# A state-space layer and a memory transformer on one core: a branch for the fallback, a last output tile in three pieces, x in half rows

## The chip, the core and the metric

The kernel runs on one core of a Trainium2 chip. The time is that of the device in microseconds for one execution; lower is better. TensorE (PE) multiplies, VectorE (DVE), ScalarE (ACT) and GpSimd (POOL) do elementwise work, SyncE (SP) issues most transfers; ACT issues a few.

## The reference

Two independent computations stand side by side in the output's last axis. Part A is a linear recurrence over 2048 steps with 1024 complex states. Part B is attention over segments of 32 tokens, 32 heads of 128, where each segment sees 8 memory rows that are the first 8 output rows of the segment before. Cut to what matters:

```python
# part A: x is (1, 2048, 1024)
Bu = einsum('bld,pd->blp', x, B_bar)
for t in range(L):
    h = Lam_bar * h + Bu[:, t, :]
y = 2.0 * einsum('blp,dp->bld', hseq, Cmat).real + x * Dskip
# part B: 64 segments of 32 rows
for s in range(n_seg):
    h = concatenate([mem, x[:, 32*s:32*s+32, :]], axis=1)
    q, k, v = (einsum('btd,dhe->bhte', h, W) for W in (Wq, Wk, Wv))
    p = softmax(where(mask, q @ k.T * scale, -1e9))
    o = einsum('bhte,hed->btd', p @ v, Wo)
    mem = o[:, :8, :]
    outs.append(o[:, 8:, :])
return concatenate([a, b], axis=-1)      # (1, 2048, 2048), bf16
```

## The kernel before

Part B is computed with guessed memory rows for all segments at once, and a check compares the guess with what came out. The check writes a flag of one number. If it is set, `general` computes part B again, segment by segment; with the inputs given it isn't. The fallback is a loop at the very end, `For_i(0, f0 * NSEG, 1)` at L1063, that runs 64 times or no time at all. Its body holds 164 matmuls, 84 of them in an inner loop over heads.

The stages, in order of time:

1. Values. Seven matmuls of constants open the program (L907). Four tiles of 128 rows of x (L371, `load_rows`) and the first block of Wv (L405, `load_wv`) come by plain transfers on two queues, SP's and ACT's. TensorE turns each x tile by eight multiplications with the identity (L378, `turn_rows`), VectorE copies the result to `b_xe`, and `v_first` multiplies it with the eight chunks of Wv (L413): two chunks after the first x tile, six matmuls after the second, ten after the third, fourteen after the fourth. The order of these is pinned. The second Wv block, four small parameter loads and the rest of x, by transposing transfers on SP (L368), are issued behind them. The rest of the values follow (L413), mixed with part A's first product (L256).
2. Part A's second product (L310) with part B's guess. In it, `zeros` stores zeros to small gaps of the scratch arrays in HBM, 24 transfers on SP.
3. Queries, keys and attention (L584, L567, L610, L628).
4. The output product (L684): 16 tiles of 128 rows, each in two halves of 512 columns, 32 heads accumulated in one PSUM tile, so 32 matmuls of 128x512 each half. `evac` copies a half to SBUF, on DVE or ACT (L77, L75), and stores both halves together on SP (L714). The last tile is treated apart: each half is copied as two quarters of 256 columns, the first by DVE and stored by SP, the second by ACT and stored by ACT (L710). The check's matmuls stand between the tiles 4 to 7 of this stage.
5. The flag is loaded into a register of each engine (L1062), then the loop at L1063.

Part of the order is written out by hand (`keep_in_program_order`), the rest is by priority of the program's order. Every transfer is given one of eight semaphores in turn and waits, before it is issued, for the transfer that had that semaphore before it, the eighth before. At the loop each engine checks and settles these semaphores, jumps over the body, and checks again.

Of the kernel before, what the change touches and what calls it, by code (L numbers as in the profile page):

```python
# [9 lines left out]
BF16 = mybir.dt.bfloat16  # L10
# [13 lines left out]
T = 2048; D = 1024; KC = 8; TT = 16  # L24
PC = 8; TB = 512; NB = 4
H = 32; E = 128; SEG = 32; M = 8; NSEG = 64; L = M + SEG
# [9 lines left out]
NM = NTL + NMX  # L36
# [280 lines left out]
class PartB:  # L317
# [32 lines left out]
    def zeros(self, pool):  # L350
        k = self.k
        z = pool.tile([32, 128], BF16, name="b_z", bufs=1)
        k.G.memset(z[:], 0.0)

        def put(dst, n):
            k.tc.keep_in_program_order(k.SP.dma_start(dst.rearrange("p (a n) -> p a n", a=4), z[0:n].unsqueeze(1).to_broadcast([n, 4, 128])))
        for hb in range(HB):
            put(self.vx[hb][64 + NMX:GX, :], GX - 64 - NMX)
            put(self.vx[hb][T + 32:NSLOT, :], 32)
            put(self.omd[NM:MT, hb * 512:(hb + 1) * 512], MT - NM)  # L360

    def load_x(self, c0, c1):

# [335 lines left out]

    def evac(self, t, half):  # L700
        k = self.k
        if t not in self.ost and t < TT - 1:
            self.ost[t] = self.p4.tile([128, D], BF16, name="b_ost", bufs=5)
        acc = self.acc.pop((t, half))
        if t == TT - 1:
            r, o = slice(t * 128, (t + 1) * 128), D + 512 * half
            for i in range(2):
                st = self.p4.tile([128, 256], BF16, name="b_oe", bufs=4)
                k.copy("vs"[i], st[:], acc[:, 256 * i:256 * i + 256])
                (k.SP if i == 0 else k.nc.scalar).dma_start(self.out[0, r, o + 256 * i:o + 256 * i + 256], st[:])  # L710
            return
        k.copy("s" if half else "v", self.ost[t][:, half * 512:half * 512 + 512], acc)
        if half:
            k.SP.dma_start(self.out[0, t * 128:(t + 1) * 128, D:2 * D], self.ost.pop(t)[:])  # L714


    def check(self):
        k = self.k; V, S, PE = k.V, k.S, k.PE
# [142 lines left out]
def kernel_main(tc, A_x, A_Lre, A_Lim, A_Bre, A_Bim, A_Cre, A_Cim, A_logdt, A_Dskip, B_x, B_mem0, B_Wq, B_Wk, B_Wv, B_Wo, out,  # L861
                force=False, dbg=None):
    with ExitStack() as ctx:
# [16 lines left out]
        with pool("p1", "right") as p1:  # L880
            tmp = a.hsp.tile([128, 2 * PC * TB], BF16, name="a_hs", bufs=4)
            w01 = a.hsp.tile([128, 2 * PC * TB], BF16, name="a_hs", bufs=4)
            wvs = {i: w01[:, 4096 * i:4096 * i + 4096].rearrange("p (a b) -> p a b", a=KC) for i in range(2)}
            st0 = a.hsp.tile([128, 2 * PC * TB], BF16, name="a_hs", bufs=4)
            b.st0 = [st0[:, 1024 * i:1024 * i + 1024].rearrange("p (a b) -> p a b", a=2) for i in range(8)]
            a.pin = b.pin = True
            a.tab = a.wp = a.btp = b.vst = p1
            a.jf = b.rall[:, 0:TB + 1]
            xr = tmp[:, 4096:8192].rearrange("p (t d) -> p t d", t=4)
            q2 = (k.SP, nc.scalar)  # L890
            for j in range(2):
                b.load_rows(0, xr, q2[j], slice(j * 512, j * 512 + 512))
                b.load_wv(0, wvs[0], KC, q2[j], [j])
            for t in range(1, 4):
                b.load_rows(t, xr, q2[t % 2])
                b.load_wv(0, wvs[0], 4, q2[1 - t % 2], [t])
            for j in range(2):
                b.load_wv(1, wvs[1], 2, q2[j], [j])
            a.load_params(tmp)
            k.SP.dma_start(tmp[0:M, 0:D], b.mem0[0])  # L900
            b.load_x(512, 1024)
            b.load_x(1024, 1536)
            b.load_x(1536, T)
            one = nc.const_aps.tensor(1.0, [128, 512], BF16)
            pw = k.ps("O")
            for i in range(7):
                k.PE.matmul(pw[:, i % 2, :], one[:, 0:128], one, start=True, stop=True)  # L907

            def values():
                yield from b.v_first(wvs[0], xr, k.SP)  # L910
                for hb, q in [(1, 0), (1, 1)] + [(hb, q) for q in range(2, 8) for hb in range(2)]:
                    yield from b.v_pair(hb, q, wvs[hb], k.SP)
                for hb in range(2, HB):
                    for q in range(8):
                        if q == 1 and hb + 1 < HB and hb + 1 not in wvs:
                            wvs[hb + 1] = b.load_wv(hb + 1)
                        yield from b.v_pair(hb, q, wvs[hb], k.SP)
            v = values()
            done = 0
            while done < 20:  # L920
                next(v); done += 1
                if done == 7:
                    a.params(p1, tmp)
                    b.init(tmp, k.ps('O')[:, 0, :])
                    a.bt = a.load_b(0)
                    a.load_x(0)
                    tabs = a.tables(0)
                if done == 18:
                    a.load_x(1)
                if done in (9, 14, 17):  # L930
                    next(tabs)
                if done in (11, 13, 15, 17, 19):
                    b.sum_x((done - 11) // 2, p1)
            a.tabs = a.ntabs
            oged = 0
            for n in range(PC * NB):
                pc, tb = n // NB, n % NB
                a.stage1(pc, tb)
                if n in (0, 1):
                    a.load_x(2 + n)  # L940
                    wvs[2 + n] = b.load_wv(2 + n)
                if tb == 1 and pc + 1 < PC:
                    nbt = a.load_b(pc + 1)
                want = 20 + 4 * (n + 1) if n < 4 else 36 + (92 * (n - 3) + 27) // 28
                half = done + 2
                while done < want:
                    next(v, None); done += 1
                    if done == half:
                        a.post(a.prev)
                while done >= 32 and oged < done // 16:  # L950
                    b.og(oged, wvs.pop(oged))
                    oged += 1
                if pc + 1 < PC:
                    if tb == 0:
                        tabs = a.tables(pc + 1)
                    else:
                        next(tabs)
                    if tb == 3:
                        a.tabs, a.bt = a.ntabs, nbt
                if n == 3:  # L960
                    a.pin = b.pin = False
                if n == 8:
                    masks(k)
                    check_consts(k)
                    dB = k.cst.tile([128, D], BF16, name="a_dB")
                    tc.keep_in_program_order(nc.scalar.dma_start(dB[:], A_Dskip.unsqueeze(0).to_broadcast([128, D])))
                if n == 28:
                    a.load_c(0, 0)
                if n == 29:
                    a.load_c(0, 1)  # L970
            a.post(a.last)
            k.V.memset(b.rall[:], 0.0)
            a.load_c(1, 0)
            a.load_c(1, 1)
# [56 lines left out]
        with pool("olb", "right", 5) as olb, pool("p4", "right") as p4:  # L1031
            b.p4 = p4
            b.olp[1] = olb
            for i in range(5):
                b.load_o(*divmod(i + 3, 4))
            for _ in b.op_some([(2, 0), (3, 0)], range(3), "S"):
                pass
            for _ in b.op_some([(0, 1), (1, 1), (2, 1), (3, 1)], range(3), "O"):
                pass
            for half in range(2):  # L1040
                for t in range(4):
                    b.op(t, half, 3)
                    b.evac(t, half)
            ck = b.check()
            for tb in range(1, 4):
                if tb < 3:
                    for q in range(4):
                        b.load_o(tb + 1, q)
                for t in range(4 * tb, 4 * tb + 4):
                    for half in range(2):  # L1050
                        for _ in b.op_some([(t, half)], range(4), "A" if tb > 1 else "S"):
                            pass
                        b.evac(t, half)
                    if tb == 1:
                        for _ in range(3):
                            next(ck, None)
            for _ in ck:
                pass
        rest.close()
        if force:  # L1060
            k.V.memset(b.flag[:], 1)
        f0 = nc.values_load(b.flag[0:1, 0:1], min_val=0, max_val=1)  # L1062
        with tc.For_i(0, f0 * NSEG, 1) as it:  # L1063
            with tc.tile_pool(name="gen", bufs=1) as gp:
                b.general(it, gp)


@with_exitstack
# [59 lines left out]
```

## Time and profile before

| what | us |
|---|---|
| median of 7 runs | 1245.96 |
| lowest, highest | 1244.84, 1247.94 |
| profiled execution, its own time | 1245.16 |
| its span, first to last instruction | 1243.5 |
| TensorE busy | 1231.3 |
| VectorE, ScalarE, GpSimd busy | 610.8, 326.6, 200.2 |
| granted TensorE clock, mean | 0.999 |

A line of the chain of waits says when a piece starts, how long it is, and what it is: work of an engine, a transfer, or issue. A line of an engine's groups gives duration and count. A busy matmul of 512 columns shows 379 ns, but the next starts 216 ns after it: they overlap, and a stretch is best counted from the chain. An engine's name with q is its sequencer, which issues and branches.

### The profile page before, as it was taken

The page shows a single profiled execution, that of the slowest core. Times are in us where ns is not written, and L with a number is a line of the kernel's source. Part 1 is how long each engine was busy: PE and PEld are TensorE (multiplying, and loading weights), DVE is VectorE, ACT ScalarE, POOL GpSimd, SP SyncE. Part 2 cuts the span into 40 slices and gives each one's busy share as a digit, 9 for nine tenths or more (in the row PEclk, how much of TensorE's full clock was granted, in tenths as well). Part 3 has the DMA queues.
Part 4 walks back from the last instruction along what each step waited for, and adds up shares of the span by engine and source line. Part 5 has one row for each costly group of instructions (what it writes and reads, how often), then busy time and mean ns, then how long its engine had stood idle before and what let it go on. Part 6 is the DMA issues. An engine that isn't in the chain of part 4 may idle for free.

```text
span 1243.5 us, 19626 instructions
## 1 busy us (share of the span) xinstructions
PE 1231.3 (99%) x8045; PEld 653.3 (53%) x8116; DVE 610.8 (49%) x1124; ACT 326.6 (26%) x755; POOL 200.2 (16%) x284
## 2 busy tenths in 40 slices
PE   9999999999999999999999999999999999999998
PEld 4444444444455445566666665565556554454443
DVE  4889999999941122444444454444444450011000
ACT  3444434444310001332332333333333330000000
POOL 2000000000032140222222222322232230000000
PEclk9999999999999999999999999999999999999999
DMA  9942232333566559577768554645575469607000
GB/s 226 266 119 68 85 94 68 102 93 79 151 191 201 149 167 170 100 150 150 148 113 182 122 131 95 129 88 87 105 139 105 72 205 237 131 18 153 17 27 18
DMA packets 305733, 153.95 MB, mean 124 GB/s; under 512 B 147048, under 2 KB 299104, under 8 KB 305640
## 3 DMA queue, kind: packets, MB, share of 16 engines
q1 hardware_dynamic: 303832, 150.69, 52.8%
q10 hardware_dynamic: 1808, 1.97, 0.5%
q8 instruction: 65, 1.06, 0.4%
q14 instruction: 28, 0.23, 0.1%
HBM read 73.70 MB, written 44.71 MB: 95 GB/s over the span
## 4 chain that ended last, share of the span: by engine, by line
PE 99%; DMA 0%; issue 0%; ACTq 0%; DVE 0%; ACT 0%
PE psP L584 33%; PE psS L684 10%; PE psP L413 9%; PE psS L413 9%; PE psO L256 9%; PE psP L684 5%; PE psP L310 4%; PE psS L310 4%; PE psP L567 4%; PE psO L628 3%; PE psS L610 3%; PE psO L684 2%; PE psP L504 1%; PE psP L730 1%; PE psO L481 1%; DMA a_hs<-in_B_x_dram 0%
## 5 line engine op out<-in xcount | busy, mean ns | idle before, releaser
L584 PE MATMUL psP<-b_xe,w 128*128 128x480 bf16 x2048 | 439.6, 366 | 0.0
L584 PEld LDWEIGHTS <-w 128*128 128x128 bf16 x2048 | 193.7, 98 | 183.5
L617 POOL TENSOR_TENSOR b_m<-b_e,maskB 99x396 bf16<-99x396 bf16 x160 | 139.6, 872 | 347.9 <-ACT b_e L613 347.9
L77 DVE CAST b_q<-psP 128x480 bf16<-128x480 f32 (+1 forms) x192 | 98.1, 532 | 145.6 <-PE psP L584 134.1
L413 PEld LDWEIGHTS <-b_xe 128*128 128x128 bf16 x1024 | 99.8, 98 | 120.8 <-DVE b_xe L77 1.3
L684 PEld LDWEIGHTS <-b_ol 128*128 128x128 bf16 x1024 | 99.3, 98 | 116.9
L75 ACT ACTIVATE b_k<-psP 128x480 bf16<-128x480 f32 x128 | 73.2, 572 | 318.4 <-PE psP L584 318.4
L613 ACT ACTIVATE b_e<-psS 99x396 bf16<-99x396 f32 x176 | 87.6, 498 | 171.3 <-PE psS L610 164.6
L635 DVE TENSOR_TENSOR b_ot<-psO,b_rall 99x512 bf16<-99x512 f32 x176 | 121.6, 691 | 6.4
L256 PE MATMUL psO<-w,a_bt 128*128 128x512 bf16 x496 | 114.7, 379 | 0.8
L684 PE MATMUL psS<-w,b_ol 128*128 128x512 bf16 x438 | 98.6, 379 | 0.6
L633 DVE RECIPROCAL b_rall<-psO 99x4 f32<-99x4 f32 x176 | 31.1, 177 | 132.9 <-PE psO L628 132.9
L413 PE MATMUL psS<-w,b_xe 128*128 128x512 bf16 x378 | 90.1, 379 | 0.4
L413 PE MATMUL psP<-w,b_xe 128*128 128x512 bf16 x376 | 89.8, 379 | 0.4
L256 PEld LDWEIGHTS <-a_bt 128*128 128x128 bf16 x512 | 49.7, 98 | 59.0
L310 PEld LDWEIGHTS <-a_hs 128*128 128x128 bf16 x512 | 49.5, 98 | 58.3
L77 DVE CAST b_ost<-psS 128x512 bf16<-128x512 f32 x13 | 9.0, 691 | 125.4 <-PE psS L684 125.4
L628 PE MATMUL psO<-b_v,b_m 99*128 99x129 bf16 x704 | 70.4, 221 | 0.0
L610 PEld LDWEIGHTS <-b_k 128*128 128x128 bf16 x704 | 50.0, 98 | 33.9 <-DVE b_k L77 0.2
L610 PE MATMUL psS<-b_q,b_k 128*128 128x99 bf16 x704 | 60.1, 208 | 0.1
L75 ACT ACTIVATE b_vst<-psS 128x512 bf16<-128x512 f32 x56 | 33.4, 597 | 97.5 <-PE psS L413 74.8
L310 PE MATMUL psP<-w,a_hs 128*128 128x512 bf16 x253 | 57.7, 379 | 0.2
(200 smaller groups left out, 1079.9 us busy)
## 6 DMA issues: line engine op xcount, KB each, us to landing
b_v<-b_vx SPq DMA_DIRECT2D x16, 1056.0 KB
b_os<-b_ot SPq DMA_DIRECT2D x16, 960.0 KB
w<-in_B_Wv_dram SPq DMA_DIRECT2D x14, 1024.0 KB
b_vx<-b_vst SPq DMA_DIRECT2D x48, 256.0 KB
w<-in_B_Wo_dram SPq DMA_DIRECT2D x12, 1024.0 KB
w<-in_B_Wq_dram SPq DMA_DIRECT2D x16, 512.0 KB
w<-in_B_Wk_dram SPq DMA_DIRECT2D x16, 512.0 KB
a_xn<-in_A_x_dram SPq DMA_DIRECT2D x32, 128.0 KB
```

Of the source, the lines that this page charges most:

```text
L75: self.S.activation(out, in_, ACT.Copy)
L77: self.V.tensor_copy(out, in_)
L256: m = PE.matmul(u[:, i, :], self.bt[:, i, c, :], self.xT[tb][:, c, :], start=(c == 0), stop=(c == KC - 1))
L310: PE.matmul(py[:], self.hs[tb][:, pc, i, tt * 128:(tt + 1) * 128], self.ct[half, i][:, pc, :], start=(pc == 0 and i == 0), stop=(pc == PC ...
L413: m = self.k.PE.matmul(p[:], self.xe[:, c, t * 128:(t + 1) * 128], w[:, c, :], start=(c == 0), stop=(c == KC - 1))
L584: PE.matmul(p[:, 0:480], w[:, i * KC + c, hh * 128:(hh + 1) * 128], self.xe[:, c, 480 * q:480 * q + 480], start=(c == 0), stop=(c == KC - 1))
L610: PE.matmul(s[:, j * GW:(j + 1) * GW], kt[:, hh, g0:g0 + 128], qt[:, hh, g0:g0 + GW], start=True, stop=True)
L613: k.S.activation(e[:], s[0:GW, 0:4 * GW], ACT.Exp, scale=float(E) ** -0.5, accum_out=self.accE[0:GW, i:i + 1])
L617: k.G.tensor_tensor(v4(m[:, 0:4 * GW]), v4(e[:]), mask[0:GW, :, :].unsqueeze(2).to_broadcast([GW, 2, 2, GW]), ALU.mult)
L628: PE.matmul(o[:, gg, cs], m[:, j * GW:j * GW + 128], vt[:, 2 * u + gg, cs], start=True, stop=True)
L635: V.tensor_tensor(ot[:, 2 * u:2 * u + 2, :].rearrange("p g (h e) -> p g h e", h=2), oa[:, :, 1:257].rearrange("p g (h e) -> p g h e", h=2) ...
L684: k.PE.matmul(self.acc[t, half], ol[:, h8, tt * 128:(tt + 1) * 128], self.wo_half(half, h), start=(h == 0), stop=(h == H - 1))
```

## The change

The fallback's loop now runs always 64 times and stands inside `tc.If(f0 != 0)`. The last output tile leaves `evac` and gets a method of its own, `last`, called with three column pieces: 0 to 512, 512 to 896, 896 to 1024. Each piece has its own 32 matmuls, one copy (ACT for the first, DVE for the others) and one store on SP. What is left of the check's generator is run in the second quarter of the output product instead of after it. The first four x tiles are loaded as two half rows each, one on each queue, and the first Wv block in eight single chunks that alternate with them. Of `zeros`' stores to `omd`, eight become six, the first three times as wide.

```diff
         def put(dst, n):
-            k.tc.keep_in_program_order(k.SP.dma_start(dst.rearrange("p (a n) -> p a n", a=4), z[0:n].unsqueeze(1).to_broadcast([n, 4, 128])))
+            k.tc.keep_in_program_order(k.SP.dma_start(dst.rearrange("p (a n) -> p a n", n=128), z[0:n].unsqueeze(1).to_broadcast([n, dst.shape[1] // 128, 128])))
         for hb in range(HB):
             put(self.vx[hb][64 + NMX:GX, :], GX - 64 - NMX)
             put(self.vx[hb][T + 32:NSLOT, :], 32)
-            put(self.omd[NM:MT, hb * 512:(hb + 1) * 512], MT - NM)
+            if hb < 6:
+                put(self.omd[NM:MT, (0, 1536, 2048, 2560, 3072, 3584)[hb]:(1536, 2048, 2560, 3072, 3584, 4096)[hb]], MT - NM)
...
     def evac(self, t, half):
         k = self.k
-        if t not in self.ost and t < TT - 1:
+        if t not in self.ost:
             self.ost[t] = self.p4.tile([128, D], BF16, name="b_ost", bufs=5)
         acc = self.acc.pop((t, half))
-        if t == TT - 1:
-            r, o = slice(t * 128, (t + 1) * 128), D + 512 * half
-            for i in range(2):
-                st = self.p4.tile([128, 256], BF16, name="b_oe", bufs=4)
-                k.copy("vs"[i], st[:], acc[:, 256 * i:256 * i + 256])
-                (k.SP if i == 0 else k.nc.scalar).dma_start(self.out[0, r, o + 256 * i:o + 256 * i + 256], st[:])
-            return
         k.copy("s" if half else "v", self.ost[t][:, half * 512:half * 512 + 512], acc)
         if half:
             k.SP.dma_start(self.out[0, t * 128:(t + 1) * 128, D:2 * D], self.ost.pop(t)[:])
+
+    def last(self, pieces):
+        k = self.k
+        for n, (c0, c1) in enumerate(pieces):
+            p = k.ps("A" if n else "S")
+            for h in range(H):
+                half, c = divmod(c0, 512)
+                k.PE.matmul(p[:, 0:c1 - c0], self.ol[NB - 1, h // 8][:, h % 8, 384:512], self.wo_half(half, h)[:, c:c + c1 - c0],
+                            start=(h == 0), stop=(h == H - 1))
+            st = self.p4.tile([128, 512], BF16, name="b_oe", bufs=3)
+            k.copy("v" if n else "s", st[:, 0:c1 - c0], p[:, 0:c1 - c0])
+            k.SP.dma_start(self.out[0, T - 128:T, D + c0:D + c1], st[:, 0:c1 - c0])
...
             q2 = (k.SP, nc.scalar)
-            for j in range(2):
-                b.load_rows(0, xr, q2[j], slice(j * 512, j * 512 + 512))
-                b.load_wv(0, wvs[0], KC, q2[j], [j])
-            for t in range(1, 4):
-                b.load_rows(t, xr, q2[t % 2])
-                b.load_wv(0, wvs[0], 4, q2[1 - t % 2], [t])
+            for t in range(4):
+                for j in range(2):
+                    b.load_rows(t, xr, q2[j], slice(j * 512, j * 512 + 512))
+                for j in range(2):
+                    b.load_wv(0, wvs[0], KC, q2[j], [2 * t + j])
             for j in range(2):
                 b.load_wv(1, wvs[1], 2, q2[j], [j])
...
-                for t in range(4 * tb, 4 * tb + 4):
+                for t in range(4 * tb, min(4 * tb + 4, TT - 1)):
...
                     if tb == 1:
                         for _ in range(3):
                             next(ck, None)
-            for _ in ck:
-                pass
+                if tb == 1:
+                    for _ in ck:
+                        pass
+            b.last([(0, 512), (512, 896), (896, D)])
         rest.close()
...
         f0 = nc.values_load(b.flag[0:1, 0:1], min_val=0, max_val=1)
-        with tc.For_i(0, f0 * NSEG, 1) as it:
-            with tc.tile_pool(name="gen", bufs=1) as gp:
-                b.general(it, gp)
+        with tc.If(f0 != 0):
+            with tc.For_i(0, NSEG, 1) as it:
+                with tc.tile_pool(name="gen", bufs=1) as gp:
+                    b.general(it, gp)
```

## The prediction

> **What bounds the kernel now.** I read the page first: span, engine shares, chain of waits.
>
> ```profile
> span 1243.5 us, 19626 instructions
> PE 1231.3 (99%) x8045; PEld 653.3 (53%) x8116; DVE 610.8 (49%) x1124; ACT 326.6 (26%) x755; POOL 200.2 (16%) x284
> q8 instruction: 65, 1.06, 0.4%
> PE 99%; DMA 0%; issue 0%; ACTq 0%; DVE 0%; ACT 0%
> ```
>
> TensorE is busy in 1231.3 of 1243.5 us and is the chain for 99%. So 12.2 us are not matmul, and only they, or the number of matmul columns, can change the time. They lie at the two ends, which the chain in order of time shows (start, length, what):
>
> ```profile
> 1.74 5.48 DMA a_hs<-in_B_x_dram
> 7.22 0.05 issue
> 7.27 0.62 PE psO L378 x8
> ...
> 9.44 0.45 PE psO L378 x8
> ```
>
> ```profile
> 1231.17 6.22 PE psP L684 x28
> 1237.39 0.02 issue
> 1237.41 0.44 DVE b_oe L77
> 1237.85 0.02 issue
> 1237.87 0.38 ACT b_oe L75
> ```
>
> At the start TensorE waits for the second x tile, issued at 1.74 and landed at 7.22; from 7.27 on it does not stop. At the end the last matmul is over at 1237.37, then VectorE copies half of the tile, then ScalarE the other half, whose store is issued at 1238.28. The span runs on to 1243.47, 6.1 us after the last matmul. What fills that stretch is in the answers for the loop's line (L1063; ns min/median/max, first and last start) and in SP's waits:
>
> ```profile
> L1063 PEldq COMPARE_BRANCH  x3: 97/196/3915, 1234.1 to 1242.5; - x3
> L1063 DVEq COMPARE_BRANCH  x3: 41/51/56, 1238.2 to 1241.8; - x3
> L1063 SPq COMPARE_BRANCH  x3: 38/38/62, 1238.4 to 1242.2; - x3
> ```
>
> ```profile
> SPq L710 <- DVE b_oe L77: 12.8, 2, 6.5
> SPq L1063 <- SPq L1063: 2.6, 2, 2.3
> ```
>
> TensorE needs 3.9 us for one branch, the jump over the fallback; it starts at 1237.57 and ends at 1241.48. Other engines jump in 0.05 us. Beside it SP waits up to 2.3 us for the last stores, the latest of which completes at 1241.27. Both reach the closing barrier within 0.2 us of each other, so neither pays without the other.
>
> **The change, part by part.** *First x tiles as halves.* Before, the second tile (256 KB) went whole on ACT's queue while SP's carried 256 KB of Wv: 1024 KB were queued up to and with it. Now it is two 128 KB halves, third on each queue: 768 KB. The data curve in 0.3 us slices adds up to 0.77 MB at 5.4, 1.07 at 6.3 and 1.40 at 7.2 us; tile two landed at 7.22, so about 350 KB more had moved than its place asks (the queues and their engines don't run level). With the same excess the 768 KB land when 1.14 MB have moved, near 6.4. TensorE is free for it at about 6.2 (two Wv matmuls start at 5.37, 0.4 us each). The next need, Wv chunks 2 and 3, is 1024 KB deep: 1.28 to 1.40 MB, 6.9 to 7.2, against 7.80 for that matmul before. Gain: 0.8 us. Bounds: 1.15 (TensorE free at 6.1 instead of 7.27) and a loss of 1.0, because the halves and single chunks are 16 transfers for 10 (SP nine issues instead of six with the second Wv block, ACT the same), at 0.35 to 0.60 us each, and every transfer waits for the landing of the eighth before it (SP's wait for an x landing before L405 was 0.8 us). Behind them on SP stand four small parameter loads (used at 20.6) and the transposed x loads, the first issued at 10.50, landed at 17.1 and first used at 22.7; on ACT the table load (1.3 us) ahead of the first copy at 12.96. These slacks of 5 us and about 5 us cover three issues more; were they gone, three issues would cost about 1.2 us. What is late next is nothing on TensorE up to 22 us: x tiles three and four, by the same count landed near 8.0 and 9.5, are needed at about 8.5 and 11; the second Wv block, landed at 13.3 in this trace, at 14.5.
>
> *Zeros.* Eight small stores to omd become six, on SP near 420 to 445 us. SP issues there take 0.33 us; TensorE runs 0.45 us pieces back to back and waits for none. Cost nothing; if SP were the limit there, a gain of 0.7 us.
>
> *The last tile.* Before: 64 matmuls of 512 columns at 0.216 us (16 in 3.45 on the chain): 13.82. After: 32 of 512 (6.91), 32 of 384 (0.162 each, 5.18), 32 of 128. For the last, the nearest row is L378, eight of 128 columns with their weight loads in 0.45: 0.056 each, 1.79. Sum 13.88: +0.06. Bounds: 0 and 1.3 (a weight load in full, 98 ns). The eviction behind the last matmul: DVE took 691 ns for 512 columns and 425 for 256, so 128 take about 292; then SP's store. Issue at 0.04 + 0.29 + 0.03 = 0.36 after the last matmul, instead of 0.91: 0.55 earlier, and one transfer behind the last matmul instead of two. The copies of the first two pieces (0.60 on ACT, about 0.56 on DVE) lie under the matmuls of the next. Their stores are issued about 8.4 and 1.2 us ahead of the end; the first is covered wholly, the second should land within a microsecond after it. The pieces' PSUM tiles were copied out half a tile earlier or more, so no piece waits for one. The check's leftover loop, moved up, costs nothing: the generator has eleven steps and is asked twelve times by then.
>
> The rows of that store shrink from 512 to 256 bytes. An undisturbed store of this kernel with 512-byte rows (issued at 1230.96) completed at 1232.54: 1.58 us. The Trainium skill, "DMA: Bandwidth & Descriptors", section Specifications, speaks against the piece: transfers under 512 bytes miss the line rate and are read, merged and written. The packets of the 512-byte store took 27 ns, eight per engine; tripled by the rule, that is 0.4 us more. By the row the store costs 1.58, by the rule 2.0. I take 1.6: half the bytes in the same number of packets, and most of the time is not data.
>
> *Branch instead of zero-trip loop.* The fallback is still jumped over, 164 matmuls with their weight loads, about 360 TensorE instructions with the loops' own. Why the jump took 3.9 us: q8 carries TensorE's code, 65 packets of 16 KB for about 16,250 instructions, one per 250. The last two before the end start at 1209.97 and 1238.55: 28.6 us, 132 matmuls with their loads. Hence TensorE jumped some 30 (give or take 15) instructions ahead of the end of a packet, and landed in the packet after the next, which had to come. The Trainium skill, "Runtime: NRT & Kernel Launch", section Instruction fetch mechanics, says the same of a branch out of the two blocks held, and by that rule alone an If saves nothing: the jump stays. (Its 128 KiB for TensorE would make the jump free; the 3915 ns decide against that.) But the last tile adds 32 matmuls and 32 weight loads ahead of the jump. It then starts some 35 into the next packet, and 360 to 390 further on is the packet that follows it, whose fetch has begun on entry, about 1.9 us before the last matmul. With the 3.9 us of this trace it is there by 2.0 after it, so the jump is no longer last. The 16 KB fetch (1.37 us) also falls mostly ahead of the last store; before, it held one of 16 DMA engines from 1238.55 to 1239.92, and its eight packets made the two last stores take 3.2 and 3.0 us.
>
> So the tail after: store issued 0.36, landed 1.94; SP's remaining steps and the closing barrier took 2.2 us after the landing at 1241.27, three of them checks of further semaphores (0.07 each) that may fall away: 1.8 to 2.2. End at 3.74 to 4.14, before 6.09. Less the 0.06: gain about 2.1 (bounds: 0 and 2.9).
>
> **Sum.** -0.8 - 2.1 = -2.9. The profiled execution took 1245.16 (1.66 around its span) and would take 1242.3; it lies 0.8 under the median, from which I get 1245.96 - 2.9 = 1243.1. What a measurement of this kernel can tell is about 0.2%, 2.5 us: the forecast lies just outside.
>
> **Rivals.** *The fetch stays* (0.20). The packet border lies elsewhere or the If's arm is laid out longer, and TensorE again waits 3.9 us behind the last matmul. For it: the border is known to 15 instructions, the If's layout not at all. Then the earlier store is hidden under the fetch, and the head alone is left, with up to 0.6 of the tail: 1244.9, no change.
>
> *The head gives nothing* (0.05): the halves wait for earlier landings, the tail is as forecast: 1243.9.
>
> *A second fetch* (0.13), the case on the other side. If the not-taken arm stands behind the fallback and a further jump leads from there over another border, TensorE pays 3.9 us twice: 3.9 - 0.8 = +3.1, 1249.1. It decides from the point where the second stall exceeds 3.3. Against it: of three branches of each engine here only one stalls, and 196 ns was enough for the last.
>
> **How the numbers follow.** Both gains: 0.62, of which 0.51 beyond 2.5 us and 0.11 within (if head or tail falls at its weak end). The fetch stays: 0.01 and 0.19. Head nothing: 0.05 within. Second fetch: 0.13 slower. Faster 0.52, same 0.35, slower 0.13. The range takes in the first three cases with their bounds, 1241.7 to 1246.0, and leaves out the second fetch; the likeliest case's own range is 1242.0 to 1244.0.
>
> **What would show it.** Right: tile two's matmuls (L378) start near 6.3, no TensorE wait over 0.5 us after; TensorE's longest branch under 2.5 us, or begun before the last matmul; the last copy 0.29 us for 128 columns; 3.7 to 4.2 us from last matmul to end; the last store within 2 us. Wrong: a branch of 3.9 us behind the last matmul, two such, Wv matmuls that wait at 7 to 11 us, or 128-column matmuls apart by more than 0.06.

## The result and the profile after

The changed kernel takes 1242.7 us (median of 13 runs, 1241.93 to 1243.54); the kernel before, run beside it, 1246.09 (33 runs, 1244.60 to 1247.98). The ratio is 0.9972, 95% interval 0.9965 to 0.9979: 3.5 us less, between 2.6 and 4.4. A repeat in a later round (`e10_after`) gave 1242.57 against 1246.52, ratio 0.9969, 0.9956 to 0.9981.

The page of the changed kernel, the lines that answer to those of before:

```profile
span 1242.3 us, 19641 instructions
PE 1231.5 (99%) x8078; PEld 655.1 (53%) x8148; DVE 610.7 (49%) x1124; ACT 325.5 (26%) x754; POOL 200.2 (16%) x284
q8 instruction: 65, 1.06, 0.4%
PE 99%; DMA 0%; issue 0%; ACT 0%; SPq 0%; DVE 0%
```

TensorE is busy for 0.2 us more and is still the whole chain. Of 12.2 us outside the matmuls 10.8 are left. The chain at the start of the changed kernel (start, length, what):

```profile
1.75 4.98 DMA a_hs<-in_B_x_dram
...
6.78 0.62 PE psO L379 x8
7.40 0.01 issue
7.41 0.59 PE psS L414 x2
...
15.07 0.61 ACT a_hs L75
15.67 1.90 PE psS L414 x8
```

And at its end:

```profile
1224.71 12.11 PE psS L718 x64
1236.82 1.80 PE psP L718 x32
1238.62 0.02 issue
1238.64 0.29 DVE b_oe L77
```

Tile two is turned at 6.78 instead of 7.27, but a new wait of 0.6 us has come in front of the matmul at 15.67 (the chain names ACT's copy, which ends in the same 0.05 us as the landing of the second Wv block, at 15.63; in other traces with these loads the block alone is named), and the last matmul ends at 1238.60, 1.23 us later than before. The span ends 3.65 us after it, instead of 6.09. The branches at the If (ns min/median/max, first and last start), then SP's waits near the end:

```profile
L1071 PEldq COMPARE_BRANCH  x1: 1712/1712/1712, 1238.0 to 1238.0; - x1
L1071 SPq COMPARE_BRANCH  x1: 58/58/58, 1239.3 to 1239.3; - x1
```

```profile
SPq L722 <- DVE b_oe L77: 5.5, 2, 4.4
SPq L1071 <- SPq L1071: 0.6, 2, 0.4
```

TensorE's branch takes 1.7 us where the loop's took 3.9, and begins half a microsecond ahead of the last matmul's end. SP waits 0.4 us at most for the last store, before 2.3.

This profiled execution took 1243.96 us, longer than all the timed runs, so it shows only 1.2 us of the 3.5. The wait that the page's list of waits puts at L468 (0.7 us at 75.6) is in none of the other traces. In the trace of `e10_after` tile two is turned at 6.29 and the last matmul ends at 1237.53, 0.16 later than before, with a tail of 3.65 again. Between these two profiles the tail repeats to 0.01 us and the opening does not; the opening is therefore sized by medians below.

### The profile page after: what moved, and what is told of

The parts are those of the page before. It is cut to its first block, busy times and chain, and to the rows that moved or that the text cites. A ratio compares the mean times of both kernels' runs of the same rounds, so it can differ in the third digit from the quotient of the medians.

```text
span 1242.3 us, 19641 instructions
## 1 busy us (share of the span) xinstructions
PE 1231.5 (99%) x8078; PEld 655.1 (53%) x8148; DVE 610.7 (49%) x1124; ACT 325.5 (26%) x754; POOL 200.2 (16%) x284
## 4 chain that ended last, share of the span: by engine, by line
PE 99%; DMA 0%; issue 0%; ACT 0%; SPq 0%; DVE 0%
PE psP L585 33%; PE psS L685 9%; PE psS L414 9%; PE psP L414 9%; PE psO L256 9%; PE psP L685 5%; PE psP L310 4%; PE psS L310 4%; PE psP L568 4%; PE psO L629 3%; PE psS L611 3%; PE psO L685 2%; PE psS L718 1%; PE psP L505 1%; PE psP L737 1%; PE psO L482 1%
## 5 line engine op out<-in xcount | busy, mean ns | idle before, releaser
L685 PEld LDWEIGHTS <-b_ol 128*128 128x128 bf16 x960 | 93.1, 98 | 109.3
L685 PE MATMUL psS<-w,b_ol 128*128 128x512 bf16 x406 | 91.6, 379 | 0.6
L310 PE MATMUL psS<-w,a_hs 128*128 128x512 bf16 x245 | 57.3, 379 | 0.6
```

What stands on the lines that cost most here:

```text
L310: PE.matmul(py[:], self.hs[tb][:, pc, i, tt * 128:(tt + 1) * 128], self.ct[half, i][:, pc, :], start=(pc == 0 and i == 0), stop=(pc == PC ...
L685: k.PE.matmul(self.acc[t, half], ol[:, h8, tt * 128:(tt + 1) * 128], self.wo_half(half, h), start=(h == 0), stop=(h == H - 1))
```

## The experiments

Twelve runs. Each is one of the two kernels with a part put back or added (`e10_after` is the changed kernel as it is); the medians come first, the reasons after. "Tail" is the time from the last matmul's end to the span's end, "jump" TensorE's longest branch at the fallback, "landed" how long after the last matmul SP saw the last store complete, "rest" what followed that.

| run | opening | last tile | way past | median (runs) | ratio to before, 95% | jump ns | landed | rest | tail |
|---|---|---|---|---|---|---|---|---|---|
| before | old | quarters | loop | see above | 1 | 3915 | 3.90 | 2.19 | 6.09 |
| after | new | 3 pieces | If | 1242.70 (13) | 0.9965 to 0.9979 | 1712 | 1.85 | 1.80 | 3.65 |
| e1_head | new | quarters | loop | 1244.83 (21) | 0.9981 to 0.9994 | 4115 | 4.11 | 2.18 | 6.29 |
| e2_tail | old | 3 pieces | If | 1245.26 (21) | 0.9982 to 0.9995 | 2278 | 1.83 | 2.32 | 4.15 |
| e3_if | old | quarters | If | 1246.38 (13) | 0.9988 to 1.0005 | 3622 | 3.61 | 2.09 | 5.70 |
| e4_pieces | old | 3 pieces | loop | 1243.50 (7) | 0.9963 to 0.9986 | 1175 | 1.83 | 2.17 | 4.01 |
| e5_loop | new | 3 pieces | loop | 1242.30 (5) | 0.9950 to 0.9977 | 1135 | 1.85 | 1.76 | 3.60 |
| e6_head_if | new | quarters | If | 1244.29 (17) | 0.9976 to 0.9991 | 3402 | 3.10 | 2.16 | 5.27 |
| e7_pad_after | new | 3 pieces | If | 1244.09 (14) | 0.9973 to 0.9989 | 3827 | 2.94 | 1.80 | 4.74 |
| e8_pad_head | new | quarters | loop | 1245.47 (13) | 0.9985 to 1.0002 | 410 | 3.50 | 2.10 | 5.60 |
| e9_mix | partly | 3 pieces | If | 1242.49 (6) | 0.9957 to 0.9981 | 1998 | 1.86 | 2.09 | 3.95 |
| e10_after | new | 3 pieces | If | 1242.57 (6) | 0.9956 to 0.9981 | 1918 | 1.85 | 1.80 | 3.65 |
| e11_mix_loop | partly | 3 pieces | loop | 1242.29 (7) | 0.9959 to 0.9982 | 1468 | 1.87 | 2.02 | 3.89 |
| e12_two | new | 2 pieces | If | 1243.95 (14) | 0.9972 to 0.9988 | 3382 | 3.01 | 1.87 | 4.88 |

The kernel before took 1246.64 beside e1 to e4, 1246.47 beside e5 to e8 and 1246.52 beside e9 to e12.

**One part alone.** e1 is the kernel before with the new loads, e2 the changed kernel with the old ones:

```diff
-            for j in range(2):
-                b.load_rows(0, xr, q2[j], slice(j * 512, j * 512 + 512))
-                b.load_wv(0, wvs[0], KC, q2[j], [j])
-            for t in range(1, 4):
-                b.load_rows(t, xr, q2[t % 2])
-                b.load_wv(0, wvs[0], 4, q2[1 - t % 2], [t])
+            for t in range(4):
+                for j in range(2):
+                    b.load_rows(t, xr, q2[j], slice(j * 512, j * 512 + 512))
+                for j in range(2):
+                    b.load_wv(0, wvs[0], KC, q2[j], [2 * t + j])
```

> The kernel before with only the new loading of the first four x tiles and of the first Wv block (halves and single chunks on both queues). Theory 'start pays': the second x tile is multiplied 0.5 us earlier or more and nothing behind it is late in the mean; 0.5 to 1.0 us faster, 1245.1 to 1245.6. Rival 'start costs': the second Wv block and the transposed x loads come later by the landings that the extra transfers wait for, as in the profile of after (TensorE 0.3 us behind at 15.7 us, 1.15 us behind at 90 us); 0.3 to 1.2 us slower, 1246.4 to 1247.3. The tail stays at 6.1 us from the last matmul to the end.

> The changed kernel with the old loading at the start: branch, pieces and the merged zero stores stay. Theory 'start pays': tail alone, 2.4 us faster than before, 1243.7. Rival 'start costs': the start of after took 0.3 to 1.2 us away, so this one is faster than after, 1241.5 to 1242.4. Tail 3.6 to 3.7 us after the last matmul by both.

e1: 0.9987, 1.6 us faster (0.8 to 2.4). e2: 0.9988, 1.5 faster (0.6 to 2.2). Their sum is the whole within the intervals. At 1245.26 e2 met neither of its expectations (1243.7, or 1241.5 to 1242.4), and its tail is 4.15 instead of 3.6 to 3.7; the place of its last store among the semaphores, told below, accounts for the tail. In e1's trace tile two is turned at 6.21, a microsecond ahead of before, but the list of TensorE's waits has a new one:

```profile
PE psS L413 <- DMA a_hs<-in_B_Wv_dram: 0.9, 1, 0.9
```

It is the matmul at 15.34, the first that reads the second Wv block. By that point the whole lead is gone: before, the same matmul started at 15.35. The tail is 6.29, with its 4.1 us jump.

e3 is the kernel before with the If, e4 the kernel before with the three pieces and the new `zeros`, the loop kept:

```diff
-        with tc.For_i(0, f0 * NSEG, 1) as it:
-            with tc.tile_pool(name="gen", bufs=1) as gp:
-                b.general(it, gp)
+        with tc.If(f0 != 0):
+            with tc.For_i(0, NSEG, 1) as it:
+                with tc.tile_pool(name="gen", bufs=1) as gp:
+                    b.general(it, gp)
```

> The kernel before with only the branch round the fallback's loop. Theory 'fetch': the jump now stands at the test, which TensorE's sequencer reached 3.2 us ahead of the last matmul's end; its 3.9 us of waiting for code end 0.7 us after the last matmul and no longer count, and the code no longer holds up the last stores: tail 4.3 to 4.6 us instead of 6.1, 1.5 to 1.8 us faster, 1244.3 to 1244.6. Rival 'store': the tail was set by the last store alone, and that is as before: no change, 1246.

> The kernel before with only the last tile in three pieces (and the merged zero stores); the zero-trip loop stays. Theory 'fetch': 64 more instructions of TensorE ahead of the jump put its target into the packet that is already on its way; the jump still comes behind the last matmul but waits under 1.7 us; tail 4.0 to 4.6 us, 1.5 to 2.1 us faster, 1244.0 to 1244.6. Rival 'store': the earlier single store brings all of the tail's 2.4 us, 1243.7. Rival 'fetch stays': the jump waits 3.9 us as before, tail 6.0, no change.

The If alone gives nothing that can be told from no change (0.9996, 0.9988 to 1.0005), and its trace says why. TensorE's branch and SP's waits in e3:

```profile
L1063 PEldq COMPARE_BRANCH  x1: 3622/3622/3622, 1233.7 to 1233.7; - x1
```

```profile
SPq L1063 <- SPq L1063: 2.5, 3, 2.2
```

The jump is as long as ever, but begins 3.4 us ahead of the last matmul's end (1237.11), since TensorE's sequencer reaches it while matmuls still stand in the queue; it is over 0.2 us after that end. So the stall of 3.9 us was removed from behind the last matmul, and the tail fell by 0.4 only: SP still waits 2.2 us for the stores.

e4, with the loop kept, gains most of these four: 0.9974 (0.9963 to 0.9986), 3.2 us. Its jump of 1.2 us ends ahead of the last store's landing, and its median of 1243.50 is nearer to the rival "store" (1243.7) than to the theory (1244.0 to 1244.6). But it does not agree with e2, which is e4 with the If and gains half as much, though the two tails differ by 0.15 us only. The profiled execution of e2 was the fastest of its 21, so its trace does not show what slowed the others. Whether the If costs something beside the old loads, or the seven runs of e4 happened to be good ones, stays open. What the pieces are worth alone is thus known only as 1.5 to 3.2 us.

**The branch taken out again, the pieces taken out again.** e5 is the changed kernel with the zero-trip loop, e6 the changed kernel with the old quarters (head and If together).

> The changed kernel with the zero-trip loop put back instead of the branch (halves, pieces and zero stores stay). Theory 'fetch and store': with the pieces the jump's target is on its way already, so the loop's own jump waits about 1.2 us behind the last matmul, under the last store; tail 4.0 us against 3.65: 0.3 to 0.4 us slower than after, 1243.1, ratio to before 0.9975. Rival 'the branch pays by itself': the loop brings back the 3.9 us of waiting and with it 1.5 us or more: 1244.2 or over.

> The changed kernel with the old last tile (quarters on two queues); halves and branch stay. Theory 'fetch and store': the jump is early but the next 16 KB packet of code, fetched behind it, still meets the last two stores; tail 5.7 us as in the profile of the branch alone: 2.0 us slower than after, 1244.6 to 1244.9, ratio to before 0.9985. Rival 'the branch pays by itself': tail 4.4, 1243.5 or less.

e5, expected 0.3 to 0.4 us slower, is at 1242.30 the equal of the changed kernel, tail 3.60. The loop's three branches of TensorE:

```profile
L1071 PEldq COMPARE_BRANCH  x3: 97/187/1135, 1236.5 to 1239.2; - x3
```

Loop or branch makes no difference that can be seen beside the pieces and the new loads. e6 shows the same from the other side: with the If and without the pieces 1244.29, 1.6 over the changed kernel, tail 5.27, although its jump (3402 ns) ends before the last matmul does.

**TensorE's code moved under the same tail.** If the packets of TensorE's code (q8) decide, then matmuls added at the very start must change the end. e7 is the changed kernel with 128 TensorE instructions more; e8 is e1 with 64 more, as many as the third piece brings:

```diff
-            for i in range(7):
-                k.PE.matmul(pw[:, i % 2, :], one[:, 0:128], one, start=True, stop=True)
+            for i in range(71):
+                k.PE.matmul(pw[:, i % 2, 0:8], one[:, 0:128], one[:, 0:8], start=True, stop=True)
```

In e8 2 of the long warm-up matmuls stay and 37 short ones are added.

> The changed kernel with the seven long opening matmuls of constants replaced by 71 short ones (8 columns): 128 more TensorE instructions ahead of the jump, which moves the jump across the point from which its target lies one packet of code further. Theory 'packet border': TensorE's branch waits 3.5 to 4.0 us again, starting 0.6 us ahead of the last matmul's end, and ends 3 us behind it; tail 4.5 to 5.2 us instead of 3.65. The opening may cost up to 0.5 us. 1243.5 to 1244.7. Rival 'length of the jump alone': the branch waits 1.7 us as in after and the tail stays at 3.65.

> The kernel with the new loading of x alone, loop and old last tile kept, and the opening's seven long matmuls replaced by two long and 37 short ones: 64 more TensorE instructions ahead of the jump, as many as the three pieces add. Theory 'packet border': the loop's jump finds its code on the way or there; its wait falls from 3.9 to under 1 us, since the border is passed 31 instructions or 3.4 us ahead of the last matmul here, and no fetch meets the last stores; tail 4.2 to 4.8 us instead of 6.1 to 6.3, 1.3 to 2.0 us faster than the loading alone, 1242.9 to 1243.5. Rival 'pieces': only the shorter last store helps; the tail stays at 6.1.

e7 has the changed kernel's tail instruction for instruction, and it goes bad. TensorE's branch and SP's waits near the end, in e7:

```profile
L1071 PEldq COMPARE_BRANCH  x1: 3827/3827/3827, 1237.4 to 1237.4; - x1
```

```profile
SPq L1071 <- SPq L1071: 1.7, 2, 1.5
```

The jump takes 3.8 us again, the last store 2.58 instead of 1.49, the tail 4.74, the median 1244.09. In e7 too SP is the last at the closing barrier, 0.5 us after TensorE, so the tail is the store's. e8 is the mirror image: its jump, the longest of three branches, takes 410 ns with the loop in place. The same two views of e8:

```profile
L1064 PEldq COMPARE_BRANCH  x3: 97/179/410, 1233.9 to 1241.5; - x3
```

```profile
SPq L1064 <- SPq L1064: 2.4, 2, 2.2
```

SP's wait for the stores is still 2.2 us, and the expected gain does not come: 1245.47, and a tail of 5.60, between the rival's 6.1 and the theory's 4.2 to 4.8. The jump was cured and the tail fell from e1's 6.29 by 0.7 only, 0.6 of it because the store landed sooner; so the jump is not what sets it. The records of the transfers of these two kernels and of the changed one say what does (queue, bytes of a packet, number, start of the first, end of the last):

```
e8  q8   16384 x1     1238.51  1239.47    TensorE's code
    q1     512 x120   1238.48  1238.84    store of the third quarter
    q1     512 x8     1239.45  1239.91
    q10    512 x120   1238.92  1239.28    store of the fourth
    q10    512 x8     1239.90  1240.16
e7  q8   16384 x1     1238.84  1239.82
    q1     256 x120   1239.11  1239.38    store of the last piece
    q1     256 x8     1239.81  1240.17
after q8 16384 x1     1237.40  1238.32
    q1     256 x128   1239.79  1240.06    store of the last piece
    q8   16384 x1     1240.58  1241.65
```

Each store is spread over 16 DMA engines, eight packets on each. Where a code packet is under way, fifteen sixteenths of the store are done in 0.3 us, and the last eight packets start when the code packet ends (in e8 those of the fourth quarter behind those of the third). The store is complete only then. In the changed kernel the store lies between two code packets, 1.5 us behind the one and 0.5 ahead of the next. Its first piece, stored nearly 7 us earlier, shows the same with a packet of queue 14, the other one that the page marks "instruction": that packet runs from 1233.27 to 1234.01, the store's last eight start at 1234.00, and it takes 2.64 us from issue to landing. In e5, where its packets have all started before the first such packet, the same store takes 1.88.

**Two pieces, and fewer loads.** e12 is the changed kernel with `b.last([(0, 512), (512, D)])`. e9 loads tiles one and two as halves and the rest as before (12 transfers ahead of the second Wv block instead of 16), e11 is e9 with the loop, e10 the changed kernel again:

```diff
-            for t in range(4):
+            for t in range(2):
                 for j in range(2):
                     b.load_rows(t, xr, q2[j], slice(j * 512, j * 512 + 512))
                 for j in range(2):
                     b.load_wv(0, wvs[0], KC, q2[j], [2 * t + j])
+            for t in range(2, 4):
+                b.load_rows(t, xr, q2[t % 2])
+                b.load_wv(0, wvs[0], 4, q2[1 - t % 2], [t])
```

> The changed kernel with the last tile in two pieces of 512 columns in place of three: 64 TensorE instructions fewer ahead of the jump, the last copy 512 columns instead of 128, so the last store is issued about 0.75 us after the last matmul and not 0.36. Theory (the tail is the later of TensorE's wait for code and of a store that a code packet holds, and both hang on where the last instructions lie against the packets): the jump starts about 4 us ahead of the last matmul's end, a 16 KB packet moves 0.3 to 2.5 us after the last matmul and meets the last store, which takes 2.4 to 3.2 us; tail 5.0 to 5.7, median about 1244.2. Rival (only the last store's issue counts, 0.4 us later, and its own 1.5 us): tail 4.0 to 4.2, median 1243.0 to 1243.3.

> The changed kernel, with tiles one and two as halves and Wv chunks 0 to 3 single, but tiles three and four whole and Wv chunks 4 to 7 in pairs, as before: 14 transfers ahead of the second Wv block in place of 18. Theory (the extra transfers push the second Wv block back, and TensorE then waits for it): the second Wv block is issued near 6.4 us, before 7.6 to 8.0; the wait of 0.3 to 0.9 us that the kernels with the new loading show near 15 us goes or falls under 0.3, and the median is 0.3 to 0.8 us under the changed kernel's, about 1242.0. Rival (a whole tile arrives at a time that varies from run to run, and tiles three and four do so now): a wait of up to 1 us for tile three near 8 us in some executions, the wait near 15 us exchanged for it, and a median within 0.3 us of the changed kernel's, or up to 0.5 above it.

> The changed kernel once more, as the neighbour of the other three. Theory: 1242.3 to 1243.0 us, tile two's turn at 6.0 to 6.8 us, TensorE's long branch begun ahead of the last matmul's end, the last store landed 1.4 to 1.6 us after its issue, the tail 3.6 to 3.7 us. Rival (the good tail of the one profile was luck): a code packet meets the last store, which then takes 2.5 to 3.2 us, and the tail is 4.5 us or longer.

> The former with six fewer loads at the start (tiles one and two as halves, the rest as before) and the zero-trip loop in place of the branch. Theory (the two edits are independent, the loop costs nothing beside the three pieces): within 0.3 us of that kernel with the branch; tail 3.6 to 4.0 us, TensorE's longest branch 1.0 to 1.3 us, ahead of the last store's landing. Rival (the loop's exit checks are on the path): 0.4 to 0.8 us slower than with the branch, tail above 4.2.

e12 came nearer to the theory (tail 5.0 to 5.7) than to the rival (4.0 to 4.2), without reaching either: tail 4.88, median 1243.95, 1.4 over its neighbour. Its jump ends just before the last matmul does, the next code packet runs from 1237.40 to 1238.57, and the store issued at 1237.47 takes 2.26 us. Fifteen of its sixteen shares had landed by 1239.25, the last at 1239.71. Of the 1.2 us by which the tail exceeds e10's, 0.40 is the later issue. About 0.4 is the larger store, by the 1.83 and 1.88 us that stores with the same rows took undisturbed (the first pieces of e11 and e5), and about 0.4 is what the code packet held. TensorE's branch and SP's waits:

```profile
L1071 PEldq COMPARE_BRANCH  x1: 3382/3382/3382, 1233.3 to 1233.3; - x1
```

```profile
SPq L1071 <- SPq L1071: 1.4, 2, 1.3
```

e9 removed the wait near 15 us from its trace: that matmul starts at 14.73, in e10 at 15.41 after the wait that its list shows:

```profile
PE psS L414 <- DMA a_hs<-in_B_Wv_dram: 0.9, 1, 0.9
```

e9's last matmul ends at 1236.83 instead of 1237.53. Yet the medians are equal, 1242.49 and 1242.57. Part of the reason is in the table: the rest after the store has grown from 1.80 to 2.09. After its wait for the last store SP goes through the eight transfer semaphores, 0.07 us each, so the store's place in that row counts. e9 issues four transfers less at the start (the expectation of e11 says six), and its last store has the fourth semaphore of the row instead of the eighth: four steps more, 0.28 us. The same holds over all the traces: rest 1.76 to 1.80 with the last semaphore (after, e5, e7, e10), 2.17 to 2.32 with the second (e2, e4). The other part is that the wait near 15 us is not in every execution: e12 has the new loads in full and does not wait there. e11 equals e9 with the branch.

None of these kernels is faster than the changed one by more than the measurement tells. A kernel with e9's loads and its last store on the row's last semaphore wasn't tried; by the traces it could give 0.3 us.

## Why the prediction was right, point by point

*The total.* -2.9 was forecast, -3.5 (2.6 to 4.4) came; 1243.1 against 1242.7. The closeness owes something to luck: by the medians the head gave 1.6 us where 0.8 was forecast, and the rest 1.5 (e2) where 2.1 was, with the range that e4 leaves open.

*The tail, -2.1.* In the profiles it is -2.44, in three terms that the prediction had: the store issued 0.36 us after the last matmul instead of 0.91 (forecast 0.36), on its way 1.49 instead of 2.99 (forecast 1.6), and 1.80 for SP's remaining steps instead of 2.19 (forecast 1.8 to 2.2). The last was right for a partly wrong reason, and its three checks of 0.07 make 2.0, not 1.8. Those checks did fall away, but not with the loop, which e5 keeps (1.76): the last store moved from the fifth of the eight semaphores to the last, by six loads more, two zero stores fewer and one last store fewer. The other 0.2 is TensorE's, which in the kernel before came to the closing barrier 0.24 us after SP, behind its jump. With the old loads the last store would have the second semaphore, as in e2 and e4; so 0.4 to 0.5 of the tail's gain hangs on the head, which is why those two have tails of 4.15 and 4.01.

*The 256-byte rows.* The store with them was seen complete after 1.49 us, undisturbed, in three executions of the changed kernel or its like (after, e5, e10), against 1.58 for one with 512-byte rows. Its packets took 18 ns where those of 512 bytes took 27. The prediction had made 2.0 us of the rule in the Trainium skill, "DMA: Bandwidth & Descriptors", Specifications, by an estimate of its own that a packet would take three times as long; nothing of this is seen here.

*The last tile's matmuls, +0.06.* The chain has 12.11 and 1.80 for its 96, sum 13.91 against 13.82: +0.09. A copy of 128 columns takes 0.29, as forecast.

*The branch.* That the jump would be still there and an If alone save nothing: e3 (no change) and e5 (loop as good as If) bear it out. Where the jump lies against the packets was forecast as some 35 instructions into a packet, so that its target, 360 to 390 on, is in the next; resumed 1.2 us after the last matmul, forecast by 2.0. e7 tests the count: 128 instructions more put the jump 163 into its packet, and 360 to 390 further on is past the end of the next one (500): 3.8 us, as it should be. e8, 64 more with the loop, is at 35 again, with its target in the next packet: 410 ns. The rule of the Trainium skill ("Runtime: NRT & Kernel Launch", Instruction fetch mechanics: a jump out of the two blocks held waits for a fetch) fits all of these, read with packets of about 250 instructions.

*What fell in it.* "Neither pays without the other" was right for the jump: in the kernel before TensorE was the last at the closing barrier by 0.24 us, in e1 by 0.08, and in the other twelve traces SP was, by 0.24 us or more. So curing the jump alone could pay a quarter of a microsecond; e3 and e8 took 0.4 and 0.7 off the tails that they stand beside (before, e1), because the store too landed sooner there, by 0.3 and 0.6. In all fourteen traces the span ends 1.76 to 2.32 us after SP saw the last store landed. What costs is the packet of code that the jump, or the straight run, calls for just when the last store goes out. The prediction had this packet as a second effect beside the jump's own length; e7 and e8 show that it weighs more. The rival "the fetch stays" was put 1.8 us over the forecast (1244.9 to 1243.1). e7 is that case and lies 1.4 over the changed kernel; 1.1 of it is the tail in its profile, the rest perhaps its altered warm-up.

*The head, -0.8.* Tile two was turned between 6.06 and 6.78 in ten traces with the new loads or a part of them, in six of them below 6.4, as forecast. The term was still mis-sized, in two ways. First, "what is late next is nothing on TensorE up to 22 us" was wrong: in four of the eight traces with the new loads in full (after, e1, e5, e10) TensorE waited 0.3 to 0.9 us at the second Wv block's first matmul, in the changed kernel until it had landed at 15.63. That also broke the prediction's own sign, no wait over 0.5 us. It read the block as landed at 13.3 and needed at 14.5; in the trace of before it landed at 14.1 and was needed at 15.35, so the slack of 1.2 us was right and both times were early. The working saw that every transfer waits for the landing of the eighth before it, and costed this at the slack of the loads behind; it did not follow the second Wv block through it, whose issue went from about 4.2 to about 7.8 us. Against the profile of before this takes the gain back, wholly in e1 and e10, not at all in e12. Second, the arrival in that profile is not the usual one. With the old loads tile two was turned at 7.27, 7.00, 5.92 and 7.85 in four traces, and these four executions ran 0.9 and 1.9 and 2.7 us below the medians of their kernels and, the last, 0.2 above. The timed runs say the same: with the old loads they spread over 2.4 to 4.2 us (e3, e2), with the new ones over 0.3 to 2.7 (e5, e8). The median gain of the head is 1.6 us (0.8 to 2.4, e1), twice the forecast. That it comes from tile two's late arrivals becoming rarer is argued from these figures, not shown: no slow execution with the old loads was profiled.

*The zeros* were never run alone; nothing in the traces speaks for a cost.

## What to carry to other kernels

Count the packets of code as traffic at the end of a program: one that runs while the last store goes out holds one sixteenth of it (1.1 us in e7), and 64 or 128 instructions more of one engine, even at the program's start, moved it here. Before a stall is taken for the bound, ask what the next engine waits for: two limits that end 0.2 us apart need two cures, and the one that shows the longest line need not be the one that pays. Where executions of one kernel differ by 2 us, a single profile can size a step that repeats from one to the next, and not one that hangs on when a load happens to arrive; for that take medians of the part alone, and enough runs of them.

## What was not expected of the hardware

An If's branch on TensorE starts ahead of the last matmul's end, by 3.4 us where the last matmuls have 512 columns (e3, e12) and by 0.55 where they have 128; the loop's jump, which has exit checks ahead of it, starts 0.2 us behind that end. The fetch of a packet ran alongside the last 32 matmuls at no visible cost: 1.80 us for them with a packet under way (after) and without one (e7).

A jump whose target is, by the count above, in a packet on its way cost 0.4 to 2.3 us, one whose target is beyond it 3.4 to 4.1, in every trace.

Loads that the program issues in the same order at the same time landed up to 1.9 us apart from one execution to the next: tile two was turned between 5.92 and 7.85 with the old loads.
